# Attention scores partly on split halves, norm products inside the next batch's scores, and other search steps in a one-core Trainium2 kernel

## The chip, the cores and the metric

The kernel runs on one core of a Trainium2 chip. The core has a matrix engine (TensorE, PE in the rows; its weight loads are PEld), a vector engine (VectorE, DVE), a scalar engine (ScalarE, ACT), a general engine (GpSimd, POOL), a queue engine (SyncE, SP) and 16 DMA engines. Each engine runs its own list of instructions in order, and semaphores make one wait for another. The metric is the device time of one execution in microseconds. Of the kernel before, three timed runs gave 1256.02, 1256.36 and 1259.71 us, with a median of 1256.36.

## The reference, cut to what matters

Four batches of N = 5056 rows and C = 256 channels go through an attention over channels, and its output through a layer of eight experts, each of which takes cap = 20224 / 8 = 2528 rows.

```python
qn = q / (norm(q, axis=1) + 1e-6);  kn = k / (norm(k, axis=1) + 1e-6)   # norms over the 5056 rows
s = kn.transpose(0, 2, 1) @ qn / tau          # 256 x 256 per batch
a = exp(s - s.max(-1)); a /= a.sum(-1) + 1e-9
x = (v @ a).reshape(20224, 256)
logits = x @ w_gate                           # 8 experts
# pairs (token, expert) in falling order of logit; a token goes to the first expert with room
out[mask_e] = relu(x[mask_e] @ w1[e]) @ w2[e]
```

## The kernel before

**Stages.** For each of the four batches the kernel adds up the raw scores k^T q in one PSUM bank, then gets the norms, a softmax, and later the value products v @ a. The value products of batch 0 lie inside batch 2's scores; the others follow the scores in a tail and in a list TODO. After that the tokens are routed by logit, and the two matrix layers of the experts run from 320 us to the end.

**Scores** (`scores`, line 302). A batch has 5 chunks; each chunk has two halves of four row groups (128 rows each), with k and q side by side in a tile `ua` or `uc`: 40 row groups per batch, 160 in all. A row group costs two float32 products of 128x128 by 128x256 (line 334), each of which the engine executes as two instructions, so four rows of the trace. For the norms ScalarE squares k and q (line 347) and VectorE adds them up (`acc_k`, `acc_q`, line 348; lines 352 and 353 fold four sums into one).

**Norms and softmax.** `norms` (line 356) turns the sums into column sums on TensorE (line 358) and copies them (`nrm`, line 361). `lengths` (line 365) takes the root on ScalarE (line 367), with small steps on GpSimd (lines 368, 371 to 373, 376) and two reciprocals on VectorE (`nd` line 370, `rn` line 375). This stands behind the first four row groups of the next batch. `softmax` (line 379) lays the factors out by two products (line 386, from `nf` of line 385) and runs some twenty vector steps, from `z` (line 391) to `ac` (line 414). `turned_a` (line 417) transposes `ac`, `gates` (line 427) multiplies it with w_gate and `logits` (line 440) forms a pack of 16 columns of logits, which VectorE transposes (line 449) and copies (line 452).

**Halves.** A value product (line 283) is done in pairs of row groups. A whole pair takes float32 products, 8 instructions. A halved pair is split first: ScalarE rounds the operand to the high half `vh` (line 259), VectorE subtracts it to get the low half `vl` (line 262), and three products of halves (high by high, low by high, high by low) take the place of each float32 one: 12 instructions. Four buffers of `vh` and of `vl` go round (AHEAD = 3, plus 1). Before, 26 of the value pairs are whole, and no row group of the scores is split.

**What sets the order.** In the attention stage the order of the code and `late` (an instruction is issued behind the newest product) decide, through the scheduler, what each engine's list is. The tables LOADS, JOBS and GATES_AT say at which chunk a load, a value chunk, a pack of logits or a gate product is put. From TODO on, an Order planner with costs per instruction places the routing steps of VectorE among the products. The routing's `route` finds, for each token, the largest logit among the experts with room (line 582), marks the expert (lines 602 to 609) and a one-hot table (line 626), and searches the cut-off by counting; `route(0)` runs beside TODO. Between TODO and the layers 27 products warm the engine (line 1313).

## Time and profile before

| what | us |
|---|---|
| median of three runs | 1256.36 |
| the profiled execution | 1257.59 |
| its span (first to last instruction) | 1255.8 |
| TensorE busy in the span | 1238.3 |
| VectorE busy | 872.7 |
| ScalarE busy | 601.0 |
| GpSimd busy | 384.5 |
| DMA, mean | 128 GB/s |

The page's first lines give the busy time of each engine over the whole span. A row of the timeline gives the start, the busy time, the engine, the line, the output and inputs with shape, the number of instructions and, in brackets, the idle time before it with what ended it. Successive products overlap, so their rate is read from the starts. A row of the windows gives a stretch, its length, then busy time and instructions of PE, PEld, DVE, ACT and POOL, the TensorE clock that was granted (1.00 is full), the DMA share and GB/s. The span has stages: scores of the four batches to 193.70 us, a tail to 221.97, TODO with the search to 311.5, the layers from 320 to the end.

### The profile page before, as it was taken

What the parts mean: (1) busy time and instruction counts of PE and PEld (TensorE: products, weight loads), DVE (VectorE), ACT (ScalarE), POOL (GpSimd) and SP (SyncE); (2) the same over time, 40 slices, a digit from 0 to 9 for tenths busy, and PEclk for the clock granted to TensorE, in tenths of its full rate; (3) what the DMA queues carried; (4) which work ended last, traced back from release to release, by engine and by line L of the source; (5) the groups of instructions that cost most, each with busy time, mean ns of one, the idle gap of its engine ahead of it and who ended that gap; (6) DMA issues with size and microseconds to landing.
All of it is one profiled execution on the core that took longest, in us unless ns stands there. A gap on an engine that the chain in (4) does not pass through costs nothing.

```text
span 1255.8 us, 24082 instructions
## 1 busy us (share of the span) xinstructions
PE 1238.3 (99%) x8779; PEld 1111.2 (88%) x8779; DVE 872.7 (69%) x2457; ACT 601.0 (48%) x1441; POOL 384.5 (31%) x690
## 2 busy tenths in 40 slices
PE   8999999999999999999999999999999999999998
PEld 6888977898888988998999899988989898898998
DVE  6688496898778778868867888887785445344431
ACT  6646652467324434434533755556554554334331
POOL 1000010000432353244343452532444434334322
PEclk9999999999999999999999999999999999999999
DMA  8999875236112134143422532341434235333301
GB/s 308 314 409 414 311 275 199 118 153 235 58 48 87 41 84 121 42 90 81 126 68 59 138 79 64 80 131 40 93 73 129 59 80 146 73 69 76 69 31 34
DMA packets 184759, 160.33 MB, mean 128 GB/s; under 512 B 150080, under 2 KB 155328, under 8 KB 180032
## 3 DMA queue, kind: packets, MB, share of 16 engines
q1 hardware_dynamic: 157712, 79.33, 22.6%
q0 software_dynamic: 17664, 58.22, 14.4%
q10 hardware_dynamic: 9264, 21.24, 4.4%
q8 instruction: 69, 1.13, 0.4%
q14 instruction: 50, 0.41, 0.1%
HBM read 99.97 MB, written 41.68 MB: 113 GB/s over the span
## 4 chain that ended last, share of the span: by engine, by line
PE 84%; DVE 6%; issue 5%; POOL 2%; DMA 2%; ACT 1%; SPq 0%; POOLq 0%; DVEq 0%; ACTq 0%
PE ph L1333 33%; PE py L1365 32%; PE px L283 7%; PE s L334 7%; PE pc L699 2%; POOL out_dram L1372 1%; PE px L446 1%; DVE acc_q L348 1%; PE pi L912 1%; DVE yy L405 1%; DVE acc_k L348 1%; DMA x_d<-xs 1%; DMA ua<-in_q_dram 1%; DVE vl L262 0%; ACT ua L1184 0%
## 5 line engine op out<-in xcount | busy, mean ns | idle before, releaser
L1333 PE MATMUL ph<-xH,ua 128*128 128x512 f32 (+3 forms) x1312 | 354.8, 388 | 0.3 <-ACT xH L1300 0.3
L1365 PE MATMUL py<-uc,hH 128*128 128x256 f32 (+1 forms) x2560 | 334.5, 279 | 0.0
L1341 DVE SCALAR_TENSOR_TENSOR hL<-ph,hH 128x512 fp32r<-128x512 f32 (+3 forms) x328 | 219.4, 670 | 162.4 <-ACT hH L1336 158.2
L1365 PEld LDWEIGHTS py<-uc,hH 128*128 128x128 f32 (+1 forms) x2560 | 312.9, 187 | 2.2
L1372 POOL DMA_INDIRECT out_dram<-y,idx x160 | 162.0, 1013 | 498.1 <-ACT y L1370 445.3
L1336 ACT ACTIVATE hH<-ph 128x512 fp32r<-128x512 f32 (+3 forms) x328 | 190.6, 582 | 206.1 <-PE ph L1333 202.1
L1333 PEld LDWEIGHTS ph<-xH,ua 128*128 128x128 f32 x1312 | 238.4, 189 | 42.8 <-ACT xH L1300 0.4
L1333 PE MATMUL ph<-xL,ua 128*128 128x512 f32 (+3 forms) x656 | 201.3, 386 | 0.1
L1370 ACT ACTIVATE y<-py 128x256 f32<-128x256 f32 (+1 forms) x160 | 61.3, 383 | 251.0 <-PE py L1365 235.1
L1225 POOL DMA_INDIRECT xg<-x_d,src x156 | 156.6, 1004 | 71.6 <-issue 33.6
L1365 PE MATMUL py<-uc,hL 128*128 128x256 f32 (+1 forms) x1280 | 178.3, 280 | 0.0
L1365 PEld LDWEIGHTS py<-uc,hL 128*128 128x128 f32 (+1 forms) x1280 | 160.2, 187 | 0.0
L1333 PEld LDWEIGHTS ph<-xL,ua 128*128 128x128 f32 x656 | 122.1, 189 | 23.3 <-DVE xL L1303 0.3
L334 PE MATMUL s<-ua 128*128 128x256 f32 x320 | 73.7, 387 | 2.6 <-DMA ua<-in_q_dram 2.6
L334 PEld LDWEIGHTS s<-ua 128*128 128x128 f32 x320 | 61.0, 193 | 14.2 <-issue 3.4
L286 ACT ACTIVATE xs<-px 128x512 f32<-128x512 f32 (+1 forms) x96 | 49.4, 528 | 49.5 <-PE px L283 47.8
L334 PE MATMUL s<-uc 128*128 128x256 f32 x320 | 71.3, 380 | 0.0
L334 PEld LDWEIGHTS s<-uc 128*128 128x128 f32 x320 | 60.3, 190 | 8.8 <-issue 0.8
L283 PE MATMUL px<-aH,vh 128*128 128x256 f32 (+1 forms) x216 | 62.7, 292 | 0.0
L283 PE MATMUL px<-aH,vl 128*128 128x256 f32 (+1 forms) x216 | 61.3, 284 | 1.1 <-DVE vl L262 0.9
L1284 DVE TENSOR_TENSOR xL<-ph,xH 128x512 fp32r<-128x512 f32 (+1 forms) x66 | 42.9, 679 | 27.8 <-ACT xH L1281 25.7
L969 ACT ACTIVATE junk<-pi,rhalf 128x160 bf16<-128x160 f32 x140 | 54.0, 391 | 15.7 <-PE pi L912 14.6
(341 smaller groups left out, 1569.5 us busy)
## 6 DMA issues: line engine op xcount, KB each, us to landing
x_d<-xs ACTq DMA_DIRECT2D x39, 512.0 KB
xq<-xg SPq DMA_DIRECT2D x500, 32.0 KB
vr<-in_vt_dram SPq DMA_DIRECT2D x14, 1024.0 KB
uc<-in_k_dram SPq DMA_DIRECT2D x18, 512.0 KB
uc<-in_q_dram SPq DMA_DIRECT2D x18, 512.0 KB
ua<-in_k_dram SPq DMA_DIRECT2D x17, 512.0 KB
ua<-in_q_dram SPq DMA_DIRECT2D x17, 512.0 KB
out_dram<-y,idx POOLq DMA_INDIRECT x160, 2.4
```

The lines of the kernel that those rows point to most:

```text
L283: mm = PE.matmul(px[:, i * C:i * C + width], lhsT=l_, rhs=a_, start=(j == 0), stop=(j == len(terms) - 1))
L286: S.activation(xs[:, t % TH:t % TH + n, 0:width], px[:, 0:n * width].rearrange("p (t c) -> p t c", t=n), AF.Copy)
L334: newest[0] = PE.matmul(sb[:, ib * C:(ib + 1) * C], lhsT=kt[:, t, ib * 128:(ib + 1) * 128], rhs=qt[:, t, :], start=(first and t == 0 and i ...
L969: S.activation(junk, pi[:, i * W:i * W + COLS], AF.Sign, bias=rhalf[:, g0 + i:g0 + i + 1], scale=-1.0, accum_out=sgn[:, g0 + i:g0 + i + 1])
L1225: P.indirect_dma_start(out=xg[:n, i, :], out_offset=None, in_=x_d, in_offset=bass.IndirectOffsetOnAxis(ap=at, axis=0))
L1284: V.tensor_tensor(xL[:, kb, 0:nt], pt[:, 0:nt], xH[:, kb, 0:nt].bitcast(F32), op=OP.subtract)
L1333: PE.matmul(ph[:, 0:nt], lhsT=l[:, w], rhs=x_[:, kb, 0:nt], start=(i == 0), stop=(i == 5))
L1336: S.activation(hH[:, fb, 0:nt], ph[:, 0:nt], AF.Relu)
L1341: V.scalar_tensor_tensor(hL[:, fb, 0:nt], ph[:, 0:nt], 0.0, hH[:, fb, 0:nt].bitcast(F32), op0=OP.max, op1=OP.subtract)
L1365: PE.matmul(py[:n, 0:C], lhsT=l[:, fb, tk], rhs=w[:, d], start=(j == 0), stop=(j == 23))
L1370: S.activation(y[:n], py[:n, 0:C], AF.Copy)
L1372: sd = P.indirect_dma_start(out=out, out_offset=bass.IndirectOffsetOnAxis(ap=idx[:n, col:col + 1], axis=0), in_=y[:n], in_offset=None)
```

## The change

**Scores.** 28 of the 160 row groups are split into halves as the value pairs are: all of (batch, chunk 0, half) = (1,0,0), (1,0,1), (2,0,0), (3,0,0) and (3,0,1), and two of four in (2,1,1), (2,2,0), (2,2,1) and (2,3,0). They take their high and low halves from the same four buffers. A split group has six half products in place of four float32 instructions.

**Norms.** The norm products of the previous batch now stand in front of row group 1 (batches 1 and 3) or 3 (batch 2) of the next batch's first half, no longer behind all four.

**Value pairs.** 20 are whole, no longer 26. The four pairs of (1,0) are split during batch 3's last chunks; pair (1,2) stays whole and is spread over the tail. All halves of `a` are made where `a` is (`keep_a`), no longer beside TODO.

**Routing.** The two reductions over experts become trees of pairwise maxima (`tallest`), the broadcast products and comparisons become one small instruction per expert in bf16, and the tables are laid out expert by expert. The copy of the logits table before the predicated copy is gone.

```diff
-CUT_FROM = 12
-CUT_TO = 40
+WHOLE = ((1, 1), (1, 2), (1, 3), (1, 4))
+WHOLE_PAIRS = ((2, 3, 2), (2, 3, 6), (2, 4, 2), (2, 4, 6))
+CUT_S = {(b, 0, h): range(TH) for b, h in ((1, 0), (1, 1), (2, 0), (3, 0), (3, 1))}
+CUT_S.update({(2, 1, 1): (2, 3), (2, 2, 0): (2, 3), (2, 2, 1): (2, 3), (2, 3, 0): (2, 3)})
+NORMS_AT = {1: 1, 2: 3, 3: 1}
...
-        "tail": [("w", (1, 2)), ("l", 3), ("l", 4), ("l", 6), ("l", 7), ("l", 5)]}
+        (2, 4): [("x", 4)], (3, 0): [("l", 0)], (3, 1): [("l", 1)], (3, 2): [("l", 2)], (3, 3): [("s", (1, 0))]}
...
+        def split_s(raw):
+            sh, sl = (vp.tile([128, 2, 2, 128], F32R, name=n, bufs=AHEAD + 1).rearrange("p a b n -> p a (b n)")
+                      for n in ("vh", "vl"))
+            S.activation(sh, raw, AF.Copy)
+            V.tensor_tensor(sl, raw, sh.bitcast(F32), op=OP.subtract)
+            return sh, sl
...
+                    split = {t: split_s(kq[:, :, t]) for t in CUT_S.get((b, c, h), ())}
                     for t in range(TH):
+                        whole = kq[:, :, t]
+                        terms = [(whole, whole)]
+                        if t in split:
+                            sh, sl = split[t]
+                            terms = [(sh, sh), (sh, sl), (sl, sh)]
+                        if first and norms_before and t == NORMS_AT[b]:
+                            late(norms_before)
                         for ib in range(2):
...
                     if first:
-                        if norms_before:
-                            late(norms_before)
...
-        job(*JOBS["tail"][0])
+        fill = halves((1, 2))
+        next(fill)
+        next(fill)
+        late(logits, 4)
+        next(fill)
+        next(fill)
         aT = late(turned_a, cur["ac"])
         late(logits, 3)
...
+    def tallest(out, rows, part, n, rate):
+        while n > 2:
+            h = (n + 1) // 2
+            yield ve(h * COLS, rate)
+            V.tensor_tensor(part[:, 0:h], rows[:, 0:h], rows[:, n - h:n], op=OP.max)
+            rows, n = part, h
+        yield ve(COLS)
+        V.tensor_tensor(out, rows[:, 0], rows[:, n - 1], op=OP.max)
...
-            V.tensor_reduce(m, L[:, 0:R].rearrange("p r c -> p c r"), axis=AX.X, op=OP.max)
+            yield from tallest(m, L, top, R, 1)
...
-            V.tensor_tensor(eq[:, 0:R], eq[:, 0:R], code9[:, 0:R, None].to_broadcast([128, R, COLS]), op=OP.mult)
+            for q in range(min(R, E - 1)):
+                V.tensor_scalar(eq[:, q], eq[:, q], float(E - q), None, op0=OP.mult)
...
-            V.copy_predicated(L2[:, 0:R - 1], keep[:, 0:R - 1, None].to_broadcast([128, R - 1, COLS]),
-                              L[:, 0:R - 1])
+            V.copy_predicated(L[:, 0:R - 1], drop[:, 0:R - 1, None].to_broadcast([128, R - 1, COLS]), L[:, 1:R])
```

VectorE, at the step from batch 0 to batch 1. `acc_q` is the last fold of batch 0's squares, `nrm`, `nd` and `rn` are the norm chain, and `nf` feeds the products that the softmax needs. Before:

```order
L353 TENSOR_TENSOR acc_q<-acc_q 128x256
L361 COPY nrm<-pc 128x4
L348 TENSOR_TENSOR acc_k<-acc_k,sq 128x1024
L370 RECIPROCAL nd<-ny 128x4
L348 TENSOR_TENSOR acc_q<-acc_q,sq 128x1024
L375 RECIPROCAL rn<-ny 128x4
L348 TENSOR_TENSOR acc_k<-acc_k,sq 128x1024
L385 TENSOR_SCALAR nf<-ident,rn 128x128 x2
```

The same place after, where `vl` out of `uc` are the low halves of batch 1's first row groups:

```order
L355 TENSOR_TENSOR acc_q<-acc_q 128x256
L303 TENSOR_TENSOR vl<-uc,vh 128x512 x4
L363 COPY nrm<-pc 128x4
L350 TENSOR_TENSOR acc_k<-acc_k,sq 128x1024
L372 RECIPROCAL nd<-ny 128x4
L303 TENSOR_TENSOR vl<-uc,vh 128x512
L377 RECIPROCAL rn<-ny 128x4
L303 TENSOR_TENSOR vl<-uc,vh 128x512 x3
L387 TENSOR_SCALAR nf<-ident,rn 128x128
L350 TENSOR_TENSOR acc_q<-acc_q,sq 128x1024
L387 TENSOR_SCALAR nf<-ident,rn 128x128
```

Four low halves stand in front of `nrm`, and the four of the second half chunk stand behind `nd` and `rn`, three of them in front of `nf`.

VectorE, at the step from batch 1 to batch 2, before and then after (`vl` out of `ua`: the low halves of batch 2's first row groups; `vl` out of `vr`: those of a value pair of batch 0):

```order
L352 TENSOR_TENSOR acc_q<-acc_q 128x512
L353 TENSOR_TENSOR acc_k<-acc_k 128x256
L353 TENSOR_TENSOR acc_q<-acc_q 128x256
L361 COPY nrm<-pc 128x4
L370 RECIPROCAL nd<-ny 128x4
```

```order
L354 TENSOR_TENSOR acc_q<-acc_q 128x512
L355 TENSOR_TENSOR acc_k<-acc_k 128x256
L355 TENSOR_TENSOR acc_q<-acc_q 128x256
L303 TENSOR_TENSOR vl<-ua,vh 128x512 x4
L363 COPY nrm<-pc 128x4
L250 TENSOR_TENSOR vl<-vr,vh 128x512
L350 TENSOR_TENSOR acc_k<-acc_k,sq 128x1024
L372 RECIPROCAL nd<-ny 128x4
```

Here the four low halves that batch 2's first scores read stand behind all the sums of batch 1.

TensorE, in the tail, from the last norm products on. `pm<-ident,ac` is `turned_a`, `pm<-wg_t,aT` a gate product, `px<-a,ub` and `px<-a,vr` whole value pairs, and 32x512 products are logits. Before:

```order
L358 MATMUL pc<-ones_f,acc_k 128x1 x2
L358 MATMUL pc<-ones_f,acc_q 128x1 x2
L283 MATMUL px<-a,ub 128x256 x8
L422 MATMUL pm<-ident,ac 128x128 x4
L386 MATMUL pc<-nf,ones_f 128x128 x2
L283 MATMUL px<-a,ub 128x256 x4
L431 MATMUL pm<-wg_t,aT 128x8 x4
L283 MATMUL px<-a,ub 128x256 x4
L283 MATMUL px<-a,vr 128x256 x16
L446 MATMUL px<-vr,g_198 32x512 x8
L422 MATMUL pm<-ident,ac 128x128 x4
L431 MATMUL pm<-wg_t,aT 128x8 x4
```

After, from the end of the halved pairs of (1,0) on (24 half products and the first `turned_a` now stand in front of the last norm products, 22 half products and a gate product behind them):

```order
L271 MATMUL px<-aH,vl 128x256
L271 MATMUL px<-a,vr 128x256 x2
L388 MATMUL pc<-nf,ones_f 128x128 x2
L271 MATMUL px<-a,vr 128x256 x6
L448 MATMUL px<-vr,g_197 32x512 x8
L271 MATMUL px<-a,vr 128x256 x8
L448 MATMUL px<-vr,g_197 32x512 x8
L424 MATMUL pm<-ident,ac 128x128 x4
L433 MATMUL pm<-wg_t,aT 128x8 x4
```

Two packs of logits stand in front of the last `turned_a`, where one stood, and three follow it, where four did.

## Rows read from the trace of the kernel before

**Rows 1.** The page's first part: busy us, share of the span, instructions.

```profile
PE 1238.3 (99%) x8779; PEld 1111.2 (88%) x8779; DVE 872.7 (69%) x2457; ACT 601.0 (48%) x1441; POOL 384.5 (31%) x690
```

**Rows 2.** Windows of batch 1's scores and of the layers (columns as told above).

```profile
54.70:85.00 30.30, 30.05 (x142) 26.07 (x140) 30.23 (x48) 18.32 (x22) 0.61 (x1) 1.00 1.02 396
...
330.00:1255.80 925.80, 919.26 (x6750) 835.06 (x6745) 616.74 (x1893) 417.50 (x1137) 359.33 (x643) 1.00 0.32 80
```

**Rows 3.** The chain that ended last, 12 to 62 us: start, us, what.

```profile
12.06 34.77 PE s L334 x160
```

**Rows 4.** Timeline of PE in TODO: first and last of 26 half products.

```profile
287.82 0.28 PE L283 MATMUL px<-aH,vl 128*128 128x256 f32 x1
...
290.76 0.28 PE L283 MATMUL px<-aH,vh 128*128 128x256 f32 x1
```

**Rows 5.** Groups by line and shape on DVE: busy us, mean ns, idle before.

```profile
L262 DVE TENSOR_TENSOR vl<-vr,vh 128x512 fp32r<-128x512 f32 x38 | 25.3, 684 | 1.8 <-ACT vh L259 1.7
```

**Rows 6.** Timeline of PE, batch 0 to batch 1.

```profile
43.22 3.62 PE L334 MATMUL s<-uc 128*128 128x256 f32 x16
...
47.48 3.70 PE L334 MATMUL s<-uc 128*128 128x256 f32 x16
...
54.18 0.68 PE L386 MATMUL pc<-nf,ones_f 128*128 128x128 f32 x4 [1.27 <-DVE nf L385]
...
59.88 2.32 PE L334 MATMUL s<-uc 128*128 128x256 f32 x10
```

**Rows 7.** Timeline of DVE, the same step.

```profile
47.66 0.16 DVE L361 COPY nrm<-pc 128x4 f32<-128x4 f32 x1 [7.49 <-PE pc L358]
...
50.76 1.23 DVE L348 TENSOR_TENSOR acc_q<-acc_q,sq 128x1024 f32<-128x1024 f32 x1 [0.35 <-ACT acc_q L344]
...
53.75 0.48 DVE L385 TENSOR_SCALAR nf<-ident,rn 128x128 f32<-128x128 f32 x2
```

**Rows 8.** Timeline of POOL, the same step.

```profile
50.78 1.27 POOL L372 TENSOR_TENSOR ny<-ny,nd 128x4 f32<-128x4 f32 x1
```

**Rows 9.** Timeline of PE, batch 1 to batch 2.

```profile
81.04 3.71 PE L334 MATMUL s<-ua 128*128 128x256 f32 x16
...
89.59 0.95 PE L431 MATMUL pm<-wg_t,aT 128*128 128x8 f32 x8
```

**Rows 10.** Timeline of DVE, end of batch 1's sums.

```profile
84.94 0.42 DVE L353 TENSOR_TENSOR acc_q<-acc_q 128x256 f32<-128x256 f32 x1
```

**Rows 11.** Timeline of DVE, batch 3 and the tail.

```profile
156.01 0.16 DVE L361 COPY nrm<-pc 128x4 f32<-128x4 f32 x1 [8.58 <-PE pc L358]
...
192.09 0.42 DVE L353 TENSOR_TENSOR acc_q<-acc_q 128x256 f32<-128x256 f32 x1
...
212.60 0.71 DVE L449 STREAM_TRANSPOSE nf<-px 128x512 f32<-128x512 f32 x1
213.34 0.27 DVE L452 COPY L<-nf 128x128 f32<-128x128 f32 x1
```

**Rows 12.** Timeline of PE, from the last norm products to TODO.

```profile
193.70 0.50 PE L358 MATMUL pc<-ones_f,acc_k 128*128 128x1 f32 x4
...
198.04 0.60 PE L422 MATMUL pm<-ident,ac 128*128 128x128 f32 x4
198.48 0.61 PE L386 MATMUL pc<-nf,ones_f 128*128 128x128 f32 x4
...
212.48 0.81 PE L422 MATMUL pm<-ident,ac 128*128 128x128 f32 x4 [0.28 <-DVE ac L414]
...
214.97 1.92 PE L446 MATMUL px<-vr,g 128*32 128x512 f32 x16
...
221.97 3.29 PE L283 MATMUL px<-a,ub 128*128 128x256 f32 x14
```

**Rows 13.** Timeline of PE between TODO and the layers.

```profile
312.21 6.43 PE L1313 MATMUL ph<-identr 128*128 128x512 f32 x27 [0.69 <-ACT xs L286]
```

**Rows 14.** Windows: the first products of the layers.

```profile
324.00:326.00 2.00, 2.00 (x11) 2.00 (x11) 1.36 (x4) 0.47 (x2) 0.85 (x3) 0.50 0.22 66
```

More of the change, by code (lines that the diff above doesn't have):

```diff
@@ L227, in attention_moe @@
     later = [(b, c, t) for b, c in TODO for t in range(0, T, 2)]
-    cut = {(0, c, t) for c in range(NCH) for t in range(0, T, 2)}
-    cut |= set(later[CUT_FROM:CUT_TO] + later[CUT_TO::2])
     def is_cut(b, c, t):
-        return (b, c, t - t % 2) in cut
+        return (b, c) not in WHOLE and (b, c, t - t % 2) not in WHOLE_PAIRS
     def keep_a(b, ac):
-        if b:
-            a_f[b] = apool.tile([128, 2, GW], F32, name="a", bufs=3)
+        if b in (1, 2):
+            a_f[b] = apool.tile([128, 2, GW], F32, name="a", bufs=2)
             S.activation(a_f[b], ac, AF.Copy)
-        if b:
-            return
-        cut_a(b, ac)
-    def cut_a(b, ac, post=None):
         aH = apool.tile([128, 2, GW], F32R, name="aH", bufs=AB)
@@ L246, in cut_a @@
         a_cut[b] = (aH, aL)
-        def low():
-            V.tensor_tensor(aL, ac, aH.bitcast(F32), op=OP.subtract)
-        if post:
-            post(low)
-        else:
-            low()
+        V.tensor_tensor(aL, ac, aH.bitcast(F32), op=OP.subtract)
     def split_v(b, c, t, post=None):
@@ L469, in halves @@
         def halves(bc):
-            halved = [t for t in range(0, T, 2) if is_cut(*bc, t)]
+            halved = [t for t in range(0, T, 2) if is_cut(*bc, t) and (*bc, t) not in cuts_v]
             for t in halved[:AHEAD]:
@@ L481, in halves, with parted @@
                 yield
-        def whole(bc):
-            for _ in halves(bc):
-                pass
+        def parted(bc):
+            for t in range(0, T, 2):
+                split_v(*bc, t)
         def job(kind, n):
-            {"x": value, "l": logits, "w": whole}[kind](n)
+            {"x": value, "l": logits, "s": parted}[kind](n)
         def load_consts():
@@ L542, in attention_moe @@
         late(gates, B - 1, cur["ac"], aT)
-        for _, n in JOBS["tail"][2:]:
+        for n in (6, 7, 5):
             late(logits, n)
@@ L568, in route @@
     def route(p, R):
[L569 removed]
+        nonlocal L, U01, asg, ne, ne2
         r = {}
@@ L611, in route @@
             Q = R if few else R + R % 2
-            flat = rtile("eq", (128, E * COLS), BF)
-            yield ve(Q * COLS)
+            oh = rtile("eq", (128, E * COLS), BF).rearrange("p (r c) -> p r c", r=E)
+            for q in range(Q):
+                yield (vi if q else ve)(COLS, 4)
+                V.tensor_scalar(oh[:, q], f, float(E - q), None, op0=OP.is_equal)
             if few:
-                oh = flat.rearrange("p (r c) -> p r c", r=E)
-                V.tensor_tensor(oh[:, 0:R], f[:, None, :].to_broadcast([128, R, COLS]),
-                                code9[:, 0:R, None].to_broadcast([128, R, COLS]), op=OP.is_equal)
                 need = rtile("need", (128, E))
@@ L1259, in turn @@
         nt = n_of(p, c)
-        if not xts:
-            ffx.tile([128, 48], F32, name="pad_x", bufs=1)
         xH = ffx.tile([128, 2, 512], F32R, name="xH")
@@ L1390, in attention_moe @@
         o.patient = True
-        cutting = [st for st in later if st in cut]
+        cutting = [st for st in later if is_cut(*st) and st not in cuts_v]
         ready = {}
@@ L1401, in cut_ahead @@
             ready[st] = unit[0]
-        for b in (2, 3):
-            cut_a(b, a_f[b], post_low)
         for b, c, t in later:
```

54 lines of the change are left out of this document (23 added, 31 removed).

## The prediction, made before the changed kernel was run

> **What bounds the kernel now.** I read the page's busy times first. TensorE is busy for 1238.3 of 1255.8 us [rows 1], so only work taken from TensorE, or waits given to it, can move the end. Then the windows, stage by stage: in batch 1's scores PE is busy for 30.05 of 30.30 us and VectorE for 30.23, so there both are full; from 330 us on PE is busy for 919.26 of 925.80 us [rows 2]. Third the timelines of the joints between the batches, where a wait of PE shows the chain behind it: 1.27 us for `nf` at batch 0 to 1 [rows 6], 0.28 us for `ac` in the tail [rows 12]. The case is this: the change takes matrix work away in a stage where the vector engine is as full as the matrix engine, and pays for it in vector work.
>
> **What the matrix engine saves.** 160 score instructions take 34.77 us [rows 3], 0.217 each; a whole row group has four, 0.869. Half products of the same 256 columns start every (290.76 - 287.82)/25 = 0.118 us [rows 4]; a split group has six, 0.706. 28 groups save 28 x 0.163 = 4.6 us. A whole value pair has 8 instructions, 1.74 us, a halved one 12 of 0.118, 1.41; six pairs save 2.0. Together 6.6 us. Half products of scores are not in the trace; with both operands new for each the price lies between 0.118 and the 0.217 of the float32 ones, which would make a split group 1.30 and lose 12 us. I take 0.118: value products also load new weights each time.
>
> **What it costs elsewhere.** Each split group needs one low half on VectorE, 0.684 us [rows 5] (0.60 from start to start when they follow each other), and a high half of the same size on ScalarE, which has slack (601.0 us busy). VectorE gets 28 x 0.60 = 17 us of new work before the tail. Where it has idle time this is free, where it is full it delays everything behind. So I go through the joints.
>
> *Batch 0 to 1.* The first four low halves lie in VectorE's 7.49 us of idle time before `nrm` [rows 7] and are free. PE does the first split group at 43.22, then the norm products (47.48 - 43.22 - 16 x 0.217 = 0.79), and is through with (1,0,0) at 46.9 in place of 47.48, 0.6 us early. The next four groups wait for ScalarE, whose list has the two squares of the first half chunk and the root in front of the high halves: first high half at about 48, low half to 49.2, so PE waits some 2.4 us. `nf` comes at about 51.9 in place of 53.75, behind three of the four low halves, and PE no longer waits for it. In sum the block that ended at 59.88 [rows 6] ends at 60.2: +0.3, where the saved work alone would make it 1.3 earlier.
>
> Here a row shows GpSimd's 4-wide product of the norm chain taking 1.27 us [rows 8], beside a VectorE sum of 1.23 us that starts 0.02 us earlier [rows 7]. The Trainium skill (SBUF — State Buffer, section "SBUF: two separate sides") says why: a VectorE instruction with two SBUF inputs and a GpSimd one that reads SBUF share a port pair as an exclusive lock. The trace agrees. The low halves have two SBUF inputs, and three stand back to back behind `rn`; by that rule the scaling of `rn` waits for them and `nf` comes 0.3 us later.
>
> *Batch 1 to 2.* From `nf` to the last sum VectorE needs 84.94 + 0.42 - 53.75 = 31.6 us [rows 7, 10], with no gap to speak of [rows 2]. From 51.9 it is done at 83.5. Only then come the four low halves of (2,0,0): 84.1 for the first. PE arrives 0.3 later than at 81.04 [rows 9], so at 81.3, and waits 2.8 us. Then 4 x 0.706, the norm products 0.79 and 16 x 0.217: the end of (2,0,1) is at 91.2 in place of 89.59 [rows 9], +1.6. Before, the scores needed nothing from VectorE here; only the norms did. What is queued behind the low halves is `nrm`, and with it the chain to `nf` and the softmax of batch 1. The other eight split groups of batch 2 save 1.3, and VectorE is at about half load there; but the value chunks of batch 0 share the four buffers and now come with their low halves behind those of the scores. I cost that at 1.3, what they save: +1.6 stays at the start of batch 3.
>
> *Batch 3 and the tail.* Eight split groups save 1.3 on PE; their low halves of the second half chunk stand behind `rn`, and I give that a wait of 0.8, the mean of none and the 1.6 us of the last joint. Scores end at 193.70 + 1.6 - 1.3 + 0.8 = 194.8. The norm products of batch 3, which followed at once [rows 12], now stand behind 24 half products (2.8) and `turned_a` (198.48 - 198.04 = 0.44): 198.1. VectorE by itself allows 197.4: it needed 192.51 - 156.01 = 36.5 us from `nrm` to the last fold [rows 11], `nrm` comes at 154.9 (a norm product placed three groups earlier, 1.6 later in all), and 10 low halves at 0.60 stand in the list. So both allow it at about the same time, 198.1 against 193.70: +4.4.
>
> From there the softmax sets the end: before, `turned_a` of batch 3 could start 212.48 - 193.70 = 18.8 us after the norm products. After, two transposes with their copies (0.71 + 0.27 [rows 11], 0.8 of new time each) stand in its list, and the products of line 388 come some 0.8 earlier: +0.8, so 198.1 + 19.6 = 217.7. PE's filler in between (the norm products 0.8, 22 half products 2.6, the four whole pairs of (1,2) 7.0, two packs of logits 3.5 and some 1.4 of small products) is done 15.3 us after the start of the norm products, at 213.4; PE waits 4 us, where it waited 0.28. From `turned_a` to TODO were 221.97 - 212.48 = 9.5 us with four packs of (221.97 - 214.97)/4 = 1.75; with three it is 7.74: TODO starts at 225.4, +3.4. Of the six pairs, two lie in TODO and save 0.7 there; the other four are in the sums above.
>
> *Routing and layers.* `route(0)` gets some 3.5 us shorter, but PE's last wait before the layers is 0.69 us for `xs`, a value tile on its way to memory [rows 13], and not for the search; I cost the gain at nothing. If the search were late after all, it would be by up to 3 us. The layers are bound by PE: nothing, give or take 1.
>
> **Sum:** +3.4 - 0.7 = +2.7 on the profiled execution's 1257.59, 1260.3. The profiled execution lies 1.23 above the median of the three runs, so 1259.1 in their terms.
>
> **The rivals.**
>
> *The saving arrives.* It takes that the low halves come in time. For it: VectorE's list has the sums in an order that could be done earlier (ScalarE has slack to deliver squares), and in the steps as summed the waits at batch 1 to 2 (1.6 net) and in the tail (4) eat it all; halving them gives 1259.1 - 2.8 = 1256.3, without them 1253.5, and with the whole 6.6 us 1249.8. Against it: the order of the lists, in which the first low half of (2,0,0) stands behind the last sum of batch 1, and 31.6 us of VectorE work without a gap ahead of it.
>
> *The clock falls.* After PE had stood still between TODO and the layers [rows 13], the granted clock of the window 324 to 326 us was 0.50 [rows 14], 1.2 GHz. Two us at half clock lose 1.0 us of matrix work; with what the row leaves out on either side I take 1.7. The new waits of 2.4, 2.8 and 4 us could do the same; the 1.27 us wait at 54.18 did not [rows 6]: the window behind it shows 1.00 [rows 2]. It decides where PE stands still for longer than that 1.27 us. One such stretch gives 1260.8, three 1264.2. This ends slower than before.
>
> *The split changes nothing in the bound.* Were PE's half products of scores as dear as 0.16, a split group would cost what a whole one does and the change would be waits alone: 1259.1 + 4.6 = 1263.7. Against it: the even spacing in [rows 4].
>
> **How the numbers follow.** The steps as summed, with about 2 us to either side from the waits of the joints: 0.50, 1259.1 (1256.5 to 1261). The clock falls once or more: 0.22, 1260.8 to 1264.2. The saving arrives for the most part: 0.24, 1250 to 1256. Dear half products: 0.04. The range 1252.0 to 1263.5 leaves out the last quarter of the saving case, where all waits vanish, and the second and third fall of the clock. A measurement of this kernel can tell 0.3%, 3.8 us, from no change: faster is under 1252.6, slower over 1260.1. Faster takes most of the saving case's lower half: 0.17. Slower takes the clock's case, the dear products and the upper quarter of the first, 0.38. The rest is 0.45.
>
> **What would show it.** Right: six half products per split group, 0.118 apart; a PE wait of 2 to 3 us for `vl` at the first group of (1,0,1) and of (2,0,0); norm products of batch 3 at about 198; a wait of 3 to 4 us for `ac` in the tail; TODO at about 225.4. Wrong: if VectorE's last sum of batch 1 ends well before 83, if TODO starts before 222, or if the windows after the waits show a clock under 1.00. If the layers' start shifts by anything else than TODO's start less 0.7, the search took part.

## The result, and the profile after

The changed kernel takes 1269.57 us (median of six runs, 1268.75 to 1271.16), the kernel before 1256.76 (six runs, 1255.79 to 1259.71): a ratio of 1.0101, 95% interval 1.0091 to 1.0111, 12.8 us slower. The forecast was slower by 2.7; the time lies 6.1 us above the upper end of the range. The profiled execution has a span of 1267.6 us against 1255.8, 11.8 more.

Where these 11.8 us arise is read off the start of the same piece of TensorE's program in both traces. (The end of the scores after is 191.17, the start of their last 32 instructions, plus the 6.91 us that such 32 take before, 186.79 to 193.70.)

| where, on TensorE | before | after | shift | shift forecast |
|---|---|---|---|---|
| batch 3, first score | 151.57 | 154.27 | +2.7 | +1.6 |
| scores end | 193.70 | 198.08 | +4.4 | +1.1 |
| norm products of batch 3 | 193.70 | 202.21 | +8.5 | +4.4 |
| `turned_a` of batch 3 | 212.48 | 221.05 | +8.6 | +5.2 |
| TODO starts | 221.97 | 232.43 | +10.5 | +3.4 |
| products behind TODO (line 1320, 1313 before) | 312.21 | 323.49 | +11.3 | +2.7 |
| first layer product | 320.89 | 333.14 | +12.3 | +2.7 |
| end of the span | 1255.8 | 1267.6 | +11.8 | +2.7 |

The page of the changed kernel, its busy times; TensorE is busy 2.6 us longer than in [rows 1], not shorter:

```profile
PE 1240.9 (98%) x8859; PEld 1111.8 (88%) x8859; DVE 877.6 (69%) x2562; ACT 619.9 (49%) x1475; POOL 380.7 (30%) x690
```

**Joint 0 to 1.** TensorE's timeline (start, duration, line, operation, idle time before it and what ended it), where the second half chunk of batch 1 begins:

```profile
48.78 0.38 PE L338 MATMUL s<-vh 128*128 128x256 f32 x1 [1.43 <-ACT vh L302]
49.59 0.39 PE L338 MATMUL s<-vl,vh 128*128 128x256 f32 x1 [0.42 <-DVE vl L303]
49.81 0.28 PE L338 MATMUL s<-vh,vl 128*128 128x256 f32 x1
49.93 0.28 PE L338 MATMUL s<-vh 128*128 128x256 f32 x1
...
51.02 0.39 PE L338 MATMUL s<-vl,vh 128*128 128x256 f32 x1 [0.45 <-DVE vl L303]
```

Half products of scores do start 0.12 apart, as those of values did [rows 4], and the new waits are 2.3 us together. `nf`, in VectorE's timeline, and the small product of the norm chain on GpSimd that it needs:

```profile
50.28 1.88 DVE L303 TENSOR_TENSOR vl<-uc,vh 128x512 fp32r<-128x512 f32 x3
52.09 0.28 DVE L387 TENSOR_SCALAR nf<-ident,rn 128x128 f32<-128x128 f32 x1
```

```profile
50.45 0.57 POOL L378 TENSOR_TENSOR rn<-rn,scale 128x4 f32<-128x4 f32 x1 [0.29 <-DVE rn L377]
```

**Joint 1 to 2.** TensorE, and the list of VectorE that it waits for; the low halves stand behind the last sum of batch 1:

```profile
83.34 0.38 PE L338 MATMUL s<-vh 128*128 128x256 f32 x1 [1.21 <-ACT vh L302]
84.69 0.38 PE L338 MATMUL s<-vl,vh 128*128 128x256 f32 x1 [0.97 <-DVE vl L303]
```

```profile
83.62 0.42 DVE L355 TENSOR_TENSOR acc_q<-acc_q 128x256 f32<-128x256 f32 x1
83.95 2.49 DVE L303 TENSOR_TENSOR vl<-ua,vh 128x512 fp32r<-128x512 f32 x4
```

**Batch 3.** Before, a pack of logits was one block: 16 instructions on a quarter of the array's columns each, four at a time, in 1.86 us. The kernel before:

```profile
159.46 0.62 PE L446 MATMUL px<-vr,g 128*32 128x512 f32 x2
159.48 0.62 PE L446 MATMUL px<-ub,g 128*32 128x512 f32 x2
...
161.32 2.86 PE L334 MATMUL s<-ua 128*128 128x256 f32 x12
```

After, packs 0 and 1 come in pieces between the split scores of batch 3:

```profile
156.68 1.04 PE L448 MATMUL px<-vr,g 128*32 128x512 f32 x2
157.65 0.39 PE L338 MATMUL s<-vh 128*128 128x256 f32 x1
157.97 0.62 PE L448 MATMUL px<-vr,g 128*32 128x512 f32 x1
157.98 0.62 PE L448 MATMUL px<-ub,g 128*32 128x512 f32 x1
158.42 0.59 PE L448 MATMUL px<-vr,g 128*32 128x512 f32 x1
158.43 0.59 PE L448 MATMUL px<-ub,g 128*32 128x512 f32 x1
158.95 0.39 PE L338 MATMUL s<-vl,vh 128*128 128x256 f32 x1
```

Each piece takes about 0.98 us up to the next score, whether it holds two instructions, four or eight; there are six such pieces (5.9 us) where two blocks were 3.7, and a lone score between two pieces takes 0.32 in place of 0.12. And VectorE's list at the same place:

```profile
155.97 0.16 DVE L363 COPY nrm<-pc 128x4 f32<-128x4 f32 x1 [0.49 <-PE pc L360]
...
157.74 0.18 DVE L372 RECIPROCAL nd<-ny 128x4 f32<-128x4 f32 x1
162.17 0.72 DVE L451 STREAM_TRANSPOSE nf<-px 128x512 f32<-128x512 f32 x1 [4.25 <-PE px L448]
162.81 0.14 DVE L377 RECIPROCAL rn<-ny 128x4 f32<-128x4 f32 x1
```

The transposition of pack 0 stands between two steps of batch 2's norm chain, and VectorE stands still for 4.25 us until the last piece of the pack is done. Its last sum of batch 3 ends at 202.4; before, at 192.5 [rows 11]:

```profile
201.99 0.42 DVE L355 TENSOR_TENSOR acc_q<-acc_q 128x256 f32<-128x256 f32 x1
```

**The tail.** TensorE, from the last norm products to TODO, and then the windows (length, busy time of PE, PEld, DVE, ACT and POOL with counts, granted clock, DMA share, GB/s):

```profile
202.21 0.58 PE L360 MATMUL pc<-ones_f,acc_k 128*128 128x1 f32 x4 [0.47 <-DVE acc_k L355]
...
216.19 1.92 PE L448 MATMUL px<-vr,g 128*32 128x512 f32 x16
221.05 0.81 PE L424 MATMUL pm<-ident,ac 128*128 128x128 f32 x4 [2.94 <-DVE ac L416]
222.55 1.22 PE L433 MATMUL pm<-wg_t,aT 128*128 128x8 f32 x8 [0.69 <-ACT aT L426]
224.26 3.64 PE L448 MATMUL px<-ua,g 128*32 128x512 f32 x16 [0.48 <-DVE g L437]
227.67 3.11 PE L448 MATMUL px<-uc,g 128*32 128x512 f32 x16
230.61 1.89 PE L448 MATMUL px<-vr,g 128*32 128x512 f32 x16
```

```profile
222.00:224.00 2.00, 1.22 (x8) 1.13 (x8) 0.00 (x0) 0.68 (x2) 0.00 (x0) 0.83 0.26 107
224.00:226.00 2.00, 1.74 (x12) 0.43 (x16) 0.89 (x2) 0.64 (x1) 0.00 (x0) 0.50 0.04 8
228.00:230.00 2.00, 2.00 (x12) 0.40 (x8) 0.96 (x2) 0.00 (x0) 0.00 (x0) 0.50 0.00 0
```

Three waits (2.94, 0.69, 0.48) lie within 6 us, and behind them the granted clock is 0.50, 1.2 GHz, for nearly 7 us: a pack takes 3.64 us, at full clock 1.89. From `turned_a` to TODO are 11.38 us where three packs at full clock need 9.49 - 1.75 = 7.74 [rows 12].

**Before the layers.** The first products of the layers wait longer:

```profile
330.97 0.25 PE L1298 MATMUL ph<-identr,xg 128*128 128x128 f32 x1 [1.04 <-issue]
332.38 0.56 PE L1298 MATMUL ph<-identr,xg 128*128 128x128 f32 x3 [1.16 <-DMA xg<-x_d,src]
```

### The profile page after: what moved, and what is told of

The parts are those of the page before. It is cut to its first block, busy times and chain, and to the rows that moved or that the text cites. A ratio compares the mean times of both kernels' runs of the same rounds, so it can differ in the third digit from the quotient of the medians.

```text
span 1267.6 us, 24409 instructions
## 1 busy us (share of the span) xinstructions
PE 1240.9 (98%) x8859; PEld 1111.8 (88%) x8859; DVE 877.6 (69%) x2562; ACT 619.9 (49%) x1475; POOL 380.7 (30%) x690
## 4 chain that ended last, share of the span: by engine, by line
PE 77%; issue 5%; DVE 3%; ACT 2%; POOL 2%; DMA 1%; POOLq 0%; DVEq 0%; ACTq 0%
PE ph L1340 32%; PE py L1372 31%; PE px L271 7%; PE s L338 3%; PE pc L711 2%; POOL out_dram L1379 1%; PE px L448 1%; PE pi L921 1%; DMA x_d<-xs 1%; DMA xg<-x_d,src 1%; DVE yy L407 1%; DVE acc_k L350 0%; ACT ua L1193 0%; PE ph L1298 0%; POOL xg L1234 0%
## 5 line engine op out<-in xcount | busy, mean ns | idle before, releaser
L271 PE MATMUL px<-aH,vh 128*128 128x256 f32 (+1 forms) x240 | 69.0, 291 | 0.6 <-ACT aH L239 0.6
L338 PE MATMUL s<-ua 128*128 128x256 f32 x288 | 67.7, 392 | 1.8 <-DMA ua<-in_q_dram 1.8
L271 PE MATMUL px<-aH,vl 128*128 128x256 f32 (+1 forms) x240 | 67.1, 285 | 1.6 <-DVE vl L250 1.4
L271 PE MATMUL px<-aL,vh 128*128 128x256 f32 (+1 forms) x240 | 67.9, 285 | 0.2 <-DVE aL L241 0.2
L338 PEld LDWEIGHTS s<-ua 128*128 128x128 f32 x288 | 55.7, 197 | 11.7 <-DMA ua<-in_q_dram 2.7
L350 DVE TENSOR_TENSOR acc_k<-acc_k,sq 128x1024 f32<-128x1024 f32 x36 | 43.9, 1219 | 15.5 <-ACT sq L349 15.0
```

The lines of the kernel that those rows point to most:

```text
L271: mm = PE.matmul(px[:, i * C:i * C + width], lhsT=l_, rhs=a_, start=(j == 0), stop=(j == len(terms) - 1))
L338: newest[0] = PE.matmul(sb[:, ib * C:(ib + 1) * C], lhsT=k_[:, 0, ib * 128:(ib + 1) * 128], rhs=q_[:, 1, :], start=(first and t == 0 and i ...
L350: V.tensor_tensor(acc, acc, sq, op=OP.add)
```

## A second measure: what the clock takes in every run

Each run lists its span and its mean granted clock. Span times (1 - clock) is the time that runs below full clock would have cost a TensorE that never waits; the clock is given to 0.001, so one run's figure is good to 0.6 us, and the mean over a kernel's runs to less. Where the runs of a kernel differ by much, taking it off brings them together: the four of the kernel without batch 3's split (1260.32 us at 0.999, 1264.36 at 0.996, 1267.61 at 0.994, 1265.75 at 0.993) spread over 7.3 us, and over 3.1 without the loss. "Rest" is the mean time less this loss. The kernels ran on different chips, and for the changed kernel and for the kernels of four or five runs the rest is good to 0.3 to 0.7 us only.

| kernel | median us | ratio, 95% interval | lost to the clock | rest |
|---|---|---|---|---|
| before (58 runs on four chips, without one whose layers took 40 us longer) | 1256.7 to 1257.6 | | 1.7 to 2.3 | 1255.0 to 1255.6 |
| after | 1269.57 | 1.0101 [1.0091, 1.0111] | 7.0 | 1262.8 |
| no split of scores | 1260.19 | 1.0026 [1.0016, 1.0036] | 5.3 | 1255.5 |
| split in batch 3 alone | 1263.98 | 1.0048 [1.0033, 1.0064] | 5.4 | 1258.4 |
| split in batches 1 and 2 alone | 1265.05 | 1.0067 [1.0051, 1.0082] | 5.7 | 1258.8 |
| logits in blocks | 1266.48 | 1.0068 [1.0052, 1.0083] | 6.3 | 1259.9 |
| value pairs in the tail's waits | 1262.67 | 1.0040 [1.0027, 1.0053] | 3.0 | 1259.5 |
| last packs all behind the gates | 1269.98 | 1.0112 [1.0092, 1.0132] | 7.3 | 1263.1 |
| before, with the routing alone | 1259.08 | 1.0018 [1.0009, 1.0028] | 1.6 | 1257.4 |
| before, with the norms alone | 1255.90 | 0.9990 [0.9981, 0.9999] | 1.6 | 1254.7 |
| the same, and pack 4 earlier | 1256.66 | 0.9994 [0.9985, 1.0003] | 1.5 | 1255.0 |

## The experiments

The theories were: the split scores themselves hold TensorE up, by their low halves and by what they push about in the lists (theory of the splits); or the changed tail does, with its longer wait and the clock behind it (theory of the clock); or the routing.

**Without any split of scores.** `CUT_S = {}` in the changed kernel; all else stays. Run first on a chip where the kernel before itself took 1297.92 us (in the trace of this run there, nearly all of the excess lies in the layers), then again on another.

> The changed kernel without any split row group of the scores (value pairs, norm placement, tail order and routing stay as changed). Changed kernel 1269.6 us, before 1256.8. Three accounts of the 12.8 us. Theory I: the two packs of logits that lie in pieces among the split scores of (3,0,1) cost TensorE 2.4 us and hold VectorE up for 4.3 us, and a fall of the clock after a wait in the tail adds 3.6. Theory J: the loss is in the waits for low halves at the joints of batches 0 to 1 and 1 to 2. Both need split scores, so both expect that most of the loss goes: norm products of batch 3 at 195 to 198 us, TODO from 222 to 225, 1257 to 1261 us. Theory R: the routing and the other order of the tail carry the loss; then 1264 us or more.

> The changed kernel without any split row group once more, for its time: the first run of it was on a chip on which the layers of the kernel before, too, took 40 us longer. Up to TODO the trace there began at 221.5 where the changed kernel has 232.4. Theory: 10 us of the 12.8 go with the splits, 1258 to 1260 us (ratio 1.001 to 1.003). Rival: behind TODO the changed routing loses more than the 0.5 to 2 us that it cost by itself: 1262 us or more.

0.9982 [0.9956, 1.0008] on the first chip, 1.0026 on the second. Norm products of batch 3 start at 192.20 (after: 202.21), TODO at 222.02. So the splits are 9.4 of the 12.8 us. By the second measure 7.3 of it are rest and 1.7 clock. The rest without splits (1255.5) is that of the kernel before: what is left, some 3 us, is the clock, which fell at 215 to 219 us in the profile.

**Without the split of batch 3.**

```diff
-CUT_S = {(b, 0, h): range(TH) for b, h in ((1, 0), (1, 1), (2, 0), (3, 0), (3, 1))}
+CUT_S = {(b, 0, h): range(TH) for b, h in ((1, 0), (1, 1), (2, 0))}
```

> The changed kernel with the eight row groups of batch 3 left whole; the splits of batches 1 and 2 stay. Theory I (logits in pieces in batch 3, VectorE held up behind them): scores of batch 3 end at 196 in place of 198.1, the last sums by 198 in place of 202.4, the norm products of batch 3 by 198; 1261 to 1266 us, the lower end if the clock then does not fall in the tail. Theory J (joints of batches 0 to 1 and 1 to 2): at most the 1.3 us that the splits of batch 3 save are lost too, so 1268 us or more.

> The changed kernel with batch 3's row groups whole, once more, for its time on a chip whose layers run as in the profile of before. By its trace TODO starts at 225.6 in place of 232.4; with no split at all it was 222.0 and 1260.2 us, with batch 3's splits alone 227.2 and 1264.0. If the parts add up: 1263 to 1264 us. If the splits of batches 1 and 2 cost what the joints show and no more, the same; if they cost nothing by themselves: 1260 us.

1.0023 [0.9995, 1.0051] on the first chip, 1.0067 on the second. Norm products at 196.22, 6.0 earlier than after.

**The split of batch 3 alone**, `((3, 0), (3, 1))` in the same line and no others.

> The changed kernel with the eight splits of batch 3 alone. Account by traces so far, at batch 3's norm products: 191.7 us with no split, 195.8 with batches 1 and 2 split, 202.2 with all. Theory I (batch 3's splits cost 6.5 us by themselves: pieces of logits between the split scores, VectorE held up behind them, the norm products behind 24 half products): norm products at 197 to 199, TODO at 227 to 229. Rival: the loss of batch 3 builds on the 4 us that batches 1 and 2 are late; alone, its split costs under 2 us: norm products by 194.

1.0048; norm products at 198.49, 6.3 later than without any split. In the column of the rest batch 3's groups cost 2.9 us, the others 3.3, all together 7.3: they add up to within 1.1.

**Packs of logits as blocks.** In the jobs of batch 3 a pack is issued with the scheduler's `late`, at one place:

```diff
-            {"x": value, "l": logits, "s": parted}[kind](n)
+            if kind == "l":
+                return late(logits, n)
+            {"x": value, "s": parted}[kind](n)
```

> The changed kernel with all 28 splits, but the packs of logits of batch 3's first chunks are issued behind the newest score product, so that each pack stands as one block of 16 instructions behind the scores of its chunk; VectorE's transposes of them then stand behind the norm chain. Theory I: the 16 instructions of a pack take 1.9 us again, VectorE does not stand still for 4.3 us before the factor rn, norm products of batch 3 3 to 5 us earlier than 202.2, 1261 to 1266 us. Rival L: TensorE then waits for the low halves of (3,0,1) instead, for 2 us and more, the pieces of logits only filled that wait, and the time stays at 1268 to 1270. Theory J: no change, 1269 us.

> The changed kernel with the packs of logits of batch 3's first chunks in blocks, once more, for its time on another chip. Its trace showed batch 3's norm products at 199.2 in place of 202.2 and TODO at 228.9 in place of 232.4, though the clock fell for a stretch at each of the first two joints there. Theory I: 1264 to 1266 us (3 to 5 faster than the changed kernel). Rival: 1268 or more.

1.0020 [0.9996, 1.0044] and 1.0068. The rest falls by 2.9 us. With the pieces, batch 3's scores took 1.7 us more than before (198.08 - 154.27 against 193.70 - 151.57) where the split was to save 1.3. In blocks they are no shorter: VectorE's 4.25 us are gone, but in their place the high and low halves of (3,0,1) are late, which the pieces had covered. TensorE of this kernel, and its window:

```profile
159.29 0.39 PE L338 MATMUL s<-vh 128*128 128x256 f32 x1 [0.73 <-ACT vh L302]
160.61 0.39 PE L338 MATMUL s<-vl,vh 128*128 128x256 f32 x1 [0.93 <-DVE vl L303]
...
162.20 0.41 PE L338 MATMUL s<-vl,vh 128*128 128x256 f32 x1
162.41 0.42 PE L338 MATMUL s<-vh,vl 128*128 128x256 f32 x1
```

```profile
162.00:164.00 2.00, 2.00 (x12) 2.00 (x11) 2.00 (x3) 1.69 (x3) 0.00 (x0) 0.51 0.97 299
```

Behind two waits of under 1 us the clock is 0.51, and half products start 0.21 apart in place of 0.12: the split saves nothing there, and the scores take 44.9 us (154.27 to 199.18, their end worked out as above) against 43.8 with the pieces. The gain lies behind the scores. VectorE's last sum ends 3.2 us earlier than in the changed kernel, and in the new order the norm products stand two half products behind the scores, at 199.42, no longer behind 26 and a transposition, at 202.21:

```profile
198.81 0.42 DVE L355 TENSOR_TENSOR acc_q<-acc_q 128x256 f32<-128x256 f32 x1
199.42 0.50 PE L360 MATMUL pc<-ones_f,acc_k 128*128 128x1 f32 x4
```

**Work in the tail's wait that nobody reads.** 12 products of `ones_f` and `ident` in front of the last `turned_a`, to keep TensorE busy:

```diff
+        def busy():
+            for _ in range(12):
+                pd = pcnt.tile([128, 512], F32, name="pc")
+                newest[0] = PE.matmul(pd[:, 0:128], lhsT=ones_f, rhs=ident, start=True, stop=True)
+        late(busy)
         aT = late(turned_a, cur["ac"])
```

> The changed kernel with 12 products of ones by the identity, which nothing reads, put into TensorE's wait of 2.9 us before the last transposes of the tail. They take some 2.9 us, as long as the wait. Theory K (the fall of the clock after this wait costs 3.6 us): granted clock 1.00 through 222 to 230 us, three packs of logits in 1.8 us each, TODO at 229 in place of 232.4, 1266 us. Rival: the clock falls anyway, because the wait of 0.7 us behind the transposes stays, or the products delay the transposes: 1269 to 1271 us.

1.0069 [1.0032, 1.0107] on the first chip. The filler was too long for its wait and the trial decides little:

```profile
220.67 6.50 PE L552 MATMUL pc<-ident,ones_f 128*128 128x128 f32 x24
...
228.29 1.21 PE L433 MATMUL pm<-wg_t,aT 128*128 128x8 f32 x8 [0.69 <-ACT aT L426]
```

The clock still fell, behind the two shorter waits. So one wait of 2.9 us is not needed for it, though the filler too kept TensorE busy for only 1.5 to 1.9 of each 2 us from 220 to 228.

**Pack 4 behind the last gates**, as in the kernel before; the four packs in one run.

> The changed kernel with one pack of logits (pack 4, of batch 2's gates) moved from the tail's filler to behind the last gate product, where it stood before the change. In the changed kernel the granted clock fell to half at 223 us, behind waits of 2.9, 0.7 and 0.5 us in a row (for ac, for aT and for g), and three packs of logits took 8.2 us in place of 5.3. Theory K2 (the fall comes from the row of waits behind the gate product, and the third one goes when a pack that needs nothing new stands there): clock 1.00 behind the gates, packs at 1.8 us each, TODO 2 to 3 us earlier than in the changed kernel although the wait for ac grows by 1.7. Rival K1 (the long wait for ac alone makes it fall): the clock falls all the same, TODO at the same place or 1 us later, since one more pack stands in the slow stretch.

1.0112, as after. The wait for `ac` became 4.46 us, and the clock fell before the gates already. Moving the pack neither caused nor cured it.

**Pairs that must be done anyhow, in those waits.** Two pairs of TODO's first value chunk are issued around the last `turned_a`, and pack 3 is issued ahead of it:

```diff
-    later = [(b, c, t) for b, c in TODO for t in range(0, T, 2)]
+    later = [(b, c, t) for b, c in TODO for t in range(0, T, 2)][2:]
...
+        late(logits, 3)
+        early = halves((1, 1))
+        with tc.issue_after(newest[0].ins):
+            next(early)
         aT = late(turned_a, cur["ac"])
-        late(logits, 3)
+        with tc.issue_after(newest[0].ins):
+            next(early)
```

> The changed kernel with two of TODO's whole value pairs in the tail's waits: 1.3 us of products in front of the last transposes (where TensorE waited 2.9 us for ac), the rest around them. Theory K3: the waits of 2.9 and 0.7 us shrink by 2 us together, the clock then stays at 1.00 or is at half for a shorter stretch, and TODO's end comes 2 to 5 us earlier: 1265 to 1267.5 us. Rival: what remains of the waits (over 1 us) still lets the clock fall, and only the 2 us are won: 1267.5 us or more.

1.0040, 7 us under the changed kernel: 4.0 of it clock, 3.3 the rest. The tail of this kernel, and a window:

```profile
222.69 0.33 PE L424 MATMUL pm<-ident,ac 128*128 128x128 f32 x1 [0.18 <-DVE ac L416]
...
226.01 1.92 PE L448 MATMUL px<-ua,g 128*32 128x512 f32 x16 [0.48 <-DVE g L437]
```

```profile
226.00:228.00 2.00, 1.99 (x20) 0.68 (x24) 0.00 (x1) 0.64 (x1) 0.00 (x0) 1.00 0.65 256
```

The waits are 0.18, 0.25 and 0.48 us, no window of the tail shows a clock under 1.00, and a pack takes 1.92 us again. So waits filled with needed work give the clock back here; how much of the 3.3 us is the waits themselves wasn't worked out.

**The same pairs and the norms in the kernel before**, no splits.

> The kernel before with the norm products moved (as in the run of that edit alone, which was 1.5 us faster than before and lost 1.7 us to a half clock in the tail) and with two of TODO's whole value pairs put into the tail's waits: one around the last transposes, one between the gate product and the logits. Theory K3 (the clock falls in the tail because of the waits of 0.3 and 0.7 us around the last transposes, and the waits can be filled with work that is needed anyway): no row with a granted clock under 1.00 between 205 and 225, TODO's end 1.7 us earlier for the clock and up to 1 us for the waits, 1253 to 1254.5 us (ratio 0.9965 to 0.998). Rival: the logits and with them the search start later, and TensorE waits for the search at the end of TODO, or the clock falls in any case: 1256 us.

1.0170 [1.0156, 1.0184]. Up to the layers it did what it should: no wait, clock 1.00 from 205 to 235 us, TODO ends at 309.89 in place of 312.21. From there to the first layer product it took 11.8 us in place of 8.7. Then a gather came late in the last expert (VectorE waits 18.7 us for its tile, where the kernel before shows no such wait), with waits of TensorE of 3.93 and 5.93 us, and the layers lost 18. Why the gather was late is open.

**The routing alone** (the routing hunks on the kernel before).

> The kernel before with the routing edits alone: trees of maxima, small instructions per expert, the new layout, no copy of the logits table. The attention stage is as before, TODO starts at 222.0. In the changed kernel TODO took 0.8 us longer than before though two of its pairs got shorter by 0.7, and from the warm-up to the first product of the layers it was 9.65 us in place of 8.68. Theory R (the routing edits cost this: more small VectorE instructions, more waits of TensorE in the search, a slower first gather): 2 to 3 us slower than before, TODO 91.5 us long or more. Rival (the later start of TODO did it): the same as before within 1 us. Third: the shorter search shortens the path, 1 to 3 us faster.

1.0018: slower by 2.3 us, and none of it is clock. In the trace 0.6 of it stands ahead of the first layer product (321.47 against 320.89); the rest was not found.

**Value pairs and norms on the old routing, without splits; and with 16 of the 28.** The 16 are (1,0,0), (3,0,0) and the eight of batch 2.

> The kernel before with the six value pairs on halves and the norm products inside the next batch's first scores alone: no score is split, routing and the order of the logits in the tail are as before. Without the split scores the changed kernel reached its last norm products at 191.7 us, 2.0 before the kernel before, but lost the gain again in the tail (clock at half behind the gates) and in TODO. Theory: with both put back, TODO starts at about 219 in place of 222.0 and is 0.7 shorter: 2.5 to 3.5 us faster than before (ratio 0.997 to 0.998). Rival: the value pairs of (1,0), which take VectorE from batch 3's sums, give it back in the tail: TODO at 221 to 222, no difference.

> The same with 16 of the 28 row groups split: (1,0,0), (3,0,0) and the eight of batch 2's middle chunks; those whose low halves stood on the path in the changed kernel, at (1,0,1), (2,0,0) and (3,0,1), are whole. Theory: where VectorE has idle time a split group saves 0.16 us: 16 x 0.16 = 2.6 us more than without splits, TODO at 217. Rival: the low halves of the scores and of the value pairs of batch 0 share four buffers and the groups of batch 2 wait for each other (1.4 us at the second value chunk in the changed kernel), and batch 3's logits slip in between the split scores again: TODO at 220 to 223.

1.0213 and 1.0266 in total, both spoilt by a late gather in the last expert (waits of 9.6 and 3.9 us in the first). Ahead of the layers they can be compared: norm products at 192.24 and 199.97, TODO at 223.69 and 230.10, where 219 and 217 were expected. In the first, the 1.5 us won at the norm products are lost in the tail: TensorE waits 1.68 us for `ac`, where it waited 0.28, the granted clock falls to 0.50, and two packs take 3.64 and 2.43 us. So what the value pairs and the norms bring together is not shown by a time of its own. Even the 16 groups, of which four in batch 1 had seemed free, move TODO back by 6.4 us.

**The norms alone**, on the kernel before:

```diff
+NORMS_AT = {1: 1, 2: 3, 3: 1}
...
+                        if first and norms_before and t == NORMS_AT[b]:
+                            late(norms_before)
...
-                        if norms_before:
-                            late(norms_before)
```

> The kernel before with one edit: the norm products stand in front of row group 1 (batches 1 and 3) or 3 (batch 2) of the next batch's first half. In the kernel without split scores the joint from batch 0 to 1 then had no wait for nf (1.27 us before), and batch 3's norm products came 2.0 us earlier. Theory: the waits of 1.3, 0.4 and 0.6 us at the two first joints go, TODO at 220 in place of 222.0, 1.5 to 2.3 us faster than before (ratio 0.9982 to 0.9988), if the clock does not fall in the tail. Rival: what is won at the joints is lost in the tail, where the wait for ac grows from 0.28 us and the clock falls: the same as before.

0.9990 [0.9981, 0.9999], 1.5 us faster than the kernel before by the medians: the one version whose interval lies below 1, though barely. By the second measure 0.4 us of it are rest and 0.7 clock. The 1.27 us wait of [rows 6] is gone. But in its profiled run the clock fell in the tail, behind the waits that the kernel before has too [rows 12]:

```profile
210.99 0.81 PE L423 MATMUL pm<-ident,ac 128*128 128x128 f32 x4 [0.28 <-DVE ac L415]
212.49 1.06 PE L432 MATMUL pm<-wg_t,aT 128*128 128x8 f32 x8 [0.69 <-ACT aT L425]
213.47 3.62 PE L447 MATMUL px<-vr,g 128*32 128x512 f32 x16
```

```profile
215.00:217.00 2.00, 2.00 (x16) 0.59 (x12) 0.00 (x0) 0.12 (x1) 0.00 (x0) 0.51 0.09 37
```

That run took 1258.09 us at a mean clock of 0.997; the median, 1255.90, was taken at 1.000.

**The norms, and pack 4 in front of the last gates**, to cover the 0.69 us wait.

> The kernel before with the norm products moved and pack 4 of the logits issued ahead of the last gate product, so that it fills the wait of 0.69 us for aT; nothing is taken from TODO. Theory K3 (the clock falls in the tail because of the waits that lie close together; the run with norm products alone had 0.28 and 0.69 us there and lost 1.7 us to the half clock): waits of 0.3 and 0.5 us remain, with 1.6 us of products between them, the clock stays at 1.00, TODO at 220.2 in place of 222.2 and 2.5 to 3.5 us faster than before (ratio 0.997 to 0.998). Rival: the clock falls behind the new wait for g as well: ratio 0.999, as with the norm products alone.

0.9994 [0.9985, 1.0003]: not told apart from the kernel before, nor better than the norms alone. The wait for `aT` is gone and the clock stayed at 1.00 in its tail, but TODO starts at 222.02, not at 220.2: batch 3's norm products came at 193.49 (with the norms alone 192.20), behind longer waits for a load and for halves in the stages ahead. The loss to the clock over all runs (1.5 against 1.6) did not fall.

## Why the prediction was right in sign and wrong in size

By the columns of the second measure the means differ by 12.5 us (the medians by 12.8): split scores 7.3, clock about 5 (7.0 less 1.7 to 2.3; 1.7 of it goes with the splits), routing 2.3, and 2.0 are given back between the routing alone and the kernel without splits (1257.4 against 1255.5), by the value pairs, the norms and the new order of the tail together. These are differences along one row of kernels, so that they add up is no check of them. By the prediction's own steps:

- *What TensorE saves: right where it can be seen.* Half products start 0.12 apart, so dear half products are ruled out. (They would have cost what whole ones do at 0.869/6 = 0.145, not at the 0.16 that was written.) The 2.0 that the six pairs were to save stands in no run by itself; with the norms and the new tail they gave 2.0.
- *Joint 0 to 1: right.* 2.3 us of waits against some 2.4; `nf` at 52.09 against 51.9; the scores behind it 0.7 later, against 0.3. The Trainium skill's rule (SBUF — State Buffer, section "SBUF: two separate sides") was used to say that the scaling of `rn` waits for three low halves on end. The Trainium skill gives the ports in that section to one instruction for as long as it lasts, and so far the trace agrees: GpSimd's product took 0.57 us beside the low halves, where one of this size took 0.20 at 50.50 us in the kernel before, with VectorE idle. That it waits for three in a row was the prediction's own step, and the trace doesn't show it: the product ended at 51.02, while the low halves ran to 52.16. It waited for one of them at most. `nf` was late because it stands behind them in the list.
- *Joint 1 to 2: right in kind, 0.7 us short.* The last sum ends at 84.0 (83.5), TensorE waits 2.2 (2.8), and (2,0,1) ends 2.3 later than before (1.6). I costed the value chunks of batch 0 at what the eight groups of batch 2 save. New waits there (0.63 for `aH`, 0.21 for `aL`, 1.43 for `vl` at 110 us) made the shift 2.7 at batch 3.
- *Batch 3: the step that failed.* "Scores end at ... 194.8. The norm products of batch 3 ... : 198.1." It was 198.1 and 202.2. TODO started 7.0 us later than forecast (232.43 against 225.4): 3.3 of that is the end of the scores, 0.8 lies between it and the norm products, 3.6 is the slow packs, and the softmax gave 0.8 back. Of the 3.3, 1.1 came from joint 1 to 2, and 2.2 arose in this step. It asked only when the low halves come, and gave that a wait of 0.8. It overlooked the packs of logits that share the stage: in pieces between split scores they take 5.9 us in place of 3.7 (the scores took 1.7 us more instead of 1.3 less), and the transposition of pack 0 stands in VectorE's list ahead of the norm chain (4.25 us still). The estimate that VectorE "by itself allows 197.4" added up busy times, 36.5 and 6.0 us from `nrm` to the last fold, and had no place for a standstill: it was 46.4 us, 155.97 to 202.41. Both engines were late alike, and TensorE waited only 0.47 for the sums. Packs in blocks give 2.9 back, at the norm products and not in the scores.
- *The tail: waits right, clock wrong.* From the norm products to `turned_a` were 18.84 us (19.6) with a wait of 2.94 (4). The fall of the clock was a rival with a chance of 0.22, at 1.7 us a fall. It came true, and the stretch was longer: 11.38 - 7.74 = 3.6 us in the profile; over all runs the clock took about 5 more than before. The reason given for setting it apart, that a 1.27 us wait had not done it, does not hold: with the norms alone the clock fell behind 0.28 and 0.69 us. The kernel before shows it too: between TODO and the half clock of [rows 14] its longest wait is 0.97 us:

```profile
320.14 0.45 PE L1291 MATMUL ph<-identr,xg 128*128 128x128 f32 x3 [0.97 <-DMA xg<-x_d,src]
```

- *Routing at nothing: wrong.* It costs 2.3 us.
- *TODO less 0.7: wrong by 1.5.* It became 0.8 longer, 0.4 of which the routing alone shows (90.61 against 90.24). The remainder wasn't traced.

Open are why the same waits let the clock fall in one run and not in another, where most of the routing's 2.3 us lies, the late gather in three of the kernels, and how the 3.3 us of the splits of batches 1 and 2 divide among the waits at the joints and in batch 2.

## What to carry to other kernels

Before adding work to a full engine, read its whole list in the new order and ask of each instruction what it waits for: one transposition of a side job, placed in front of a chain, stopped VectorE for as long as seven of the added low halves take. Products that use a quarter of the array's columns belong together; scattered among full ones two packs cost 5.9 us instead of 3.7, without what the scores between them lost. A wait on TensorE is paid a second time where the clock falls behind it, so a wait is best filled with work that has to be done anyhow, and the mean clock of every timed run tells whether that worked better than one profile can.

## What the runs showed of the hardware

- The clock fell to half for some 3 to 7 us behind waits as short as 0.28 and 0.69 us, in the profile of one kernel (the norms alone) and not in another's with the same tail (before); in one kernel behind 0.73 and 0.93. Two runs of one kernel differ by 7 us (1260.32 at 0.999, 1267.61 at 0.994), of which the second measure puts some 6 down to the clock.
- 24 instructions for 12 products of 128 float32 columns took 6.5 us, 0.27 each, at a granted clock of 1.00, where the four instructions of line 388 take 0.61 us together. What made them dear (the one weight tile, or that each starts and stops its own sum) wasn't tried.
- On one chip the layers of the same kernel took 40 us longer (before: 1297.92, 31 runs, mean clock 0.992). The clock accounts for 8 to 9 of it (10.6 lost against 1.7 to 2.3 elsewhere); the rest is open.
